# Zeros written by VectorE for the idle products, six early scores in a group, and products in the first four places of the first round

## The chip, the cores and the metric

The kernel runs on one core of one Trainium2 chip. Its time is the device time of one execution in microseconds. Engines are named as in the profile: PE is TensorE (PEld its weight loads), DVE is VectorE, ACT is ScalarE, POOL is GpSimd, SP is SyncE, which issues the loads and stores.

## The reference

A layer norm, then full attention over 32 heads of width 16 and a bilinear gated network on the same normalised rows; their product is added to the input. S = 2048 tokens, D = 512, F = 1792, all in float32.

```
xn = layernorm(x)
q, k, v = split(xn @ wqkv)                  # 32 heads of 16
p = softmax(q k^T / 4);  s = (p v) @ wo
g = silu(((xn @ w_gate) * (xn @ w_up)) @ w_down)
out = x + s * g
```

## The kernel before

Products are split: each float32 operand is cut into a high and a low part, and three products (high-high, high-low, low-high) are summed, so a 128x512 tile with a depth of 512 takes twelve matmuls. The kernel has three stages.

**Start and early stage** (`early`, line 707 on). Four tiles of x are loaded and normalised, transposed on TensorE (`ln_turn`, L246), and K, Q and V are projected from them (`full`, L267). To have something on TensorE while the first tiles are being normalised there are *idle products*, `warm` (L730): matmuls of the identity with a tile of zeros named `acc`, four ahead of the first transposes and three between the first and the second transposes. A float32 matmul shows as two in the trace, hence eight and six. The identity and the zeros are written by POOL, the zeros last of its set-up.

The 252 projection products of the early stage run as one stream, numbered by `n`. At some values of `n` other work is put in: statistics, normalisations, transposes of the remaining x tiles, and, by the table `EARLY`, *early scores* (`score`, L610 and L612). A score is a matmul of a 48-row piece of Q with K into one bank of PSUM; two scores that follow each other lie in the lower and the upper half of the array. VectorE then takes the maximum of each row of the bank (`TENSOR_REDUCE mx<-s`). Scores of a query block must all be done before its exponentials; 64 of them make a block, after which `maxima` reduces them once more (L616 to L621) and stores them. In all 86 scores (`LEAD`) run in the early stage, so that the scores stay 86 ahead of the exponentials from there on. The banks of this stage are four for scores (tag `s`), two for transposes and idle products (`x`), two for projections (`f`).

**Main part.** It is a chain of *places* (`position`). In a place stand one product for an exponential (`expo`, t, L632; ScalarE takes the exponential, L634) and one score (L610). After eight places or so, as the loop at the end of `body` decides, follows a *block* of weighted values (`block`, pv, L645). Between the places the *filler* puts other products (the rest of the projections, the gated network), as pairs of half-array matmuls (`pair`, L286 and L290). `spread(n)` shares the products of a round out to n gaps, `part` issues one gap's share. In the main part three banks (`s`) hold scores, three (`st`) hold t and pv, two (`misc`) the filler's sums.

The first round differs: four places stand ahead of the loop, without filler; the loop's first turn adds eight more, with the filler's share in six gaps. Then comes the first block.

**End** (`ending`): the output projection, the gate, the sum and the stores.

What sets the order: TensorE, ScalarE, VectorE and GpSimd execute in the order in which the program is written (a manual schedule), with waits only on data and on banks. SP issues all transfers from one queue, in program order.

Of the kernel before, what the change touches and what calls it, by code (L numbers as in the profile page):

```python
# [11 lines left out]
F32 = mybir.dt.float32  # L12
# [7 lines left out]
P = 128  # L20
# [11 lines left out]
LEAD = 86  # L32
CYCLES = 240
AHEAD = range(1, 5)
# [2 lines left out]
EBUFS = 11  # L37
HBUFS = 2
QBUFS = 2
EARLY = [66, 75, 84, 93] + [104 + 37 * n // 4 for n in range(17)]  # L40
EARLY_BUFS = {"s": 4, "x": 2, "f": 2}
BUFS = {"st": 3, "s": 3, "misc": 2}
LOWER, UPPER = slice(0, 64), slice(64, P)
# [5 lines left out]
def body(ctx, tc, x, wqkv, wo, wg, wu, wd, out):  # L49
    nc = tc.nc  # L50
    x = x.rearrange("b s d -> (b s) d")
# [19 lines left out]
    pool, sync = Tied(nc.gpsimd), Tied(nc.sync)  # L71

    def dma(dst, src):
        sync.dma_start(dst, src)
# [5 lines left out]
    keep = ctx.enter_context(tc.tile_pool(name="keep", bufs=1))  # L80
# [6 lines left out]
    OD = [dram.tile([H, 32, 512], F32, name=f"OD{c}") for c in range(NC)]  # L87
    YD = [dram.tile([P, 4, D], F32, name=f"YD{c}") for c in range(NC)]

    ident = keep.tile([P, P], F32, name="ident")  # L90
    make_identity(nc, ident)
    ks = [keep.tile([P, 2, S], F32R, name="ks0")]
# [9 lines left out]
    def ones_columns(tts):  # L102
        pool.memset(V[:, tts, DH:H * VW:VW], 1.0)
        pool.memset(V[:, tts, H * VW:], 1.0)

    ones_columns(slice(0, 8))
    idle = keep.tile([P, 512], F32, name="acc", bufs=2)
    pool.memset(idle, 0.0)

    fst = {}  # L110

# [5 lines left out]
    def psum(tag, name):  # L117
        ps, bufs = fst["ps"]
        return ps.tile([P, 512], F32, tag=tag, name=name, bufs=bufs[tag])
# [28 lines left out]
    def etile():  # L148
        return ep.tile([P, 512], F32, name="e", bufs=EBUFS)
# [15 lines left out]
    def wtile(name):  # L165
        return keep.tile([P, ND, P], F32 if name[-1] == "r" else F32R, name=name, bufs=1 if name[-1] == "r" else 2)
# [23 lines left out]
    def load_x(tt):  # L190
        dma(tokens(tt), x[tt * P:(tt + 1) * P])
# [406 lines left out]
            for pr in range(2):  # L598
                dma(k[b:b + 2, pr].bitcast(F32), ones)

    def score(n, other):

        i, r = divmod(n, 4 * NT)
        r, j = divmod(r, 4)
        j ^= other
        kc, t = divmod(r, 4)
        b, pr = 64 * (j % 2), j // 2
        k = ks[(i // NC) % 2]
        o = psum("s", f"s{i}_{r}_{j}")
        nc.tensor.matmul(o, QS[i][b:b + KB, pr, t * P:(t + 1) * P],  # L610
                         k[b:b + KB, pr, kc * 512:(kc + 1) * 512], start=True, stop=True)
        nc.vector.tensor_reduce(MX[i][:, j, t, kc:kc + 1], o, axis=AX.X, op=OP.max)  # L612
# [94 lines left out]
    def early():  # L707

        nc.scalar.activation(look, eps[0:1], AF.Sqrt)
        for tt in range(4):  # L710
            load_x(tt)
        wraw = []
        for which in (1, 0):
            wraw.append(wtile(f"w{which}r"))
            dma(wraw[-1], wqkv[:, which * D:which * D + P].rearrange("(d p) f -> p d f", p=P))
        norm["raws"] = raws = [etile() if d < 3 else part_tile() for d in range(ND)]
        for d in range(ND):
            dma(raws[d], wqkv[d * P:(d + 1) * P, 2 * D:])
        for tt in range(4, NT):
            load_x(tt)  # L720

        def ahead(m):
            fst["qk", m] = qk_weights(m, 1), qk_weights(m, 0)

        def exp_table(_):
            nc.scalar.activation(look, eps[0:1], AF.Exp)

        def warm(n):
            for _ in range(n):
                nc.tensor.matmul(psum("x", "warm"), ident, idle, start=True, stop=True)  # L730

        warm(4)
        first = (0, 1), (2, 3)
        for tts in first:
            ln_open(tts)
        ln_stats(0)
        ln_stats(1)
        ln_root(first[0])
        ln_scale(first[0])
        ln_apply(0)  # L740
        ln_apply(1)
        ln_stats(2)
        ln_stats(3)
        ln_turn(0)
        ln_turn(1)
        warm(3)
        ln_root(first[1])
        ln_scale(first[1])
        ln_apply(2)
        last = ln_apply(3)  # L750
        ln_low(0)
        ln_low(1)
        ln_turn(3)
        ln_turn(2)
        ln_low(3)
        ln_low(2)
        wk, wq = [split_raw(f"w{which}", raw, last) for which, raw in zip((1, 0), wraw)]
        wv = [[etile().bitcast(F32R) for _ in range(ND)] for _ in range(2)]
        for d in range(ND):
            nc.scalar.activation(wv[0][d], raws[d], AF.Copy)  # L760
            pool.tensor_tensor(wv[1][d], raws[d], wv[0][d], op=OP.subtract)

        def k(c):
            yield from qk_proj(wk, 0, 1, c, "f")
            load_k(0, [c])

        def q(c):
            yield from qk_proj(wq, 0, 0, c, "f" if c else "x")
            load_q(c)

        def v(*tts):
            for tt in tts:
                yield from v_proj(wv, tt, "f")

        at = {n: [] for n in range(253)}
        for c, stats, apply, turns in ((1, (0, 2, 4, 6), (26, 26, 26, 26), (38, 42, 46, 50)),
                                       (2, (16, 20, 26, 27), (60, 60, 62, 62), (70, 74, 79, 83)),
                                       (3, (30, 34, 36, 38), (73, 73, 85, 85), (100, 106, 112, 118))):
            for t in range(4):
                for n, fn in ((stats[t], ln_stats), (apply[t], ln_apply), (turns[t], ln_turn)):  # L780
                    at[n].append((fn, 4 * c + t))
        for tts, n, root, scale in ((tuple(range(4, 8)), 0, 13, 25), (tuple(range(8, NT)), 16, 52, 53)):
            at[n].insert(0, (ln_open, tts))
            at[root].append((ln_root, tts))
            at[scale].insert(0, (ln_scale, tts))
        at[190].append((ones_rows, ks[0]))
        at[150].append((exp_table, None))
        at[205].append((ahead, 1))
        at[130] += [(ones_columns, slice(8, NT)), (other_keys, None)]
        fst["v"] = v_proj(wv, NT - 1, "st")  # L790
        gens = [k(0), q(0), v(0, 1, 2), k(1), q(1), v(3), k(2), v(4, 5), k(3), v(*range(6, NT - 1))]
        scored = 0
        stream = (n for g in gens for n in g)
        for n in range(253):
            for fn, arg in at[n]:
                fn(arg)
            if n in EARLY:
                for _ in range(4 if n != EARLY[-1] else LEAD - scored):
                    score(scored, 0)
                    scored += 1  # L800
                if scored == 64:
                    maxima(0)
            next(stream, None)
        assert scored == LEAD
        return wq
# [132 lines left out]
    TOTAL = NU * NT * 4  # L938

    with tc.manual_schedule(engines=ORDERED):  # L940
        with banks_of(EARLY_BUFS):
            fil = Filler(filler(early()), spread)
        ctx.enter_context(banks_of(BUFS))
        run(fst["v"])
        q = 0
        while q < 4:
            position(q)
            q += 1
        for b in range(NU * NT // 2):
            if fil.done:  # L950
                parts = iter([3, 2, 3, 2, 2, 2, 1, 2])
                fil = Filler(ending(), lambda n: next(parts))
            work = fil.begin()
            if b >= NU * NT // 2 - 2:
                last = TOTAL - 4 * (NU * NT // 2 - 1 - b)
            else:
                fits = min(9, max(7, int(2.6 + 0.62 * work))) if q + LEAD < TOTAL and work else 8
                need = 8 * (b + 1)
                last = min(max(q + fits, need + AHEAD[0]), need + AHEAD[-1], TOTAL - 4)
            count = last - q  # L960
            fil.spread(max(2, count - 2))
            for k in range(count):
                if k == count - 1:
                    run_all(gates)
                position(q)
                q += 1
                if 0 < k < count - 1 or count < 3:
                    fil.part()
            if b < NU * NT // 2 - 1:
                values([ready.pop(2 * b), ready.pop(2 * b + 1)])  # L970
        run_all(before_values)
        run_all(gates)
        while heads:
            step_small(heads)
        block([ready.pop(NU * NT - 2), ready.pop(NU * NT - 1)])
        run_all(behind_values)
        flush()
        while fil.left or not fil.done:
            now[0] += 1
            prepare()  # L980
            if not fil.left:
                fil.fetch()
            for _ in range(fil.left):
                next(fil.gen)
            fil.left = 0
            fil.fetch()
            flush()
# [17 lines left out]
```

## Time and profile before

| | us |
|---|---|
| median of three runs | 1714.24 (1713.63 to 1714.4) |
| the profiled execution, whole | 1715.28 |
| its span | 1713.4 |
| first idle product | 2.70 |
| first transposes on TensorE | 9.05 |
| first early scores | 31.80 |
| first place of the main part | 102.50 |
| first block of weighted values | 109.65 |

The times in the trace count from the start of the span. A row of the timeline reads: start, length (both in us), engine, line and operation, written tile and read tiles, shape, count, and in brackets how long the engine had been idle before it and what it waited for. Consecutive instructions of one kind are merged into one row with their count. The length of a matmul in the trace is longer than the distance to the next one, since matmuls overlap; so the pace of TensorE is read from the distances between starts.

### The profile page before, as it was taken

How to read it: one execution, taken by the hardware profiler on the slowest of the kernel's cores; microseconds unless marked ns; L12 is line 12 of the kernel's file. 1: busy time of each engine (PE TensorE's matmuls, PEld its weight loads, DVE VectorE, ACT ScalarE, POOL GpSimd, SP SyncE). 2: the span in 40 equal slices, each digit the busy share in tenths (PEclk: the TensorE clock that was granted, in tenths of full speed). 3: DMA queues.
4: the chain of work that ended last, by engine and by line, in shares of the span. 5: the costliest groups of instructions: out<-in, count | busy, mean ns of one | idle time of the engine just before them, and what ended most of it. 6: DMA issues, size and time to landing. Idle time of an engine off the chain costs nothing. (4 is left out here: it accounts for less than half of the span.)

```text
span 1713.4 us, 35012 instructions
## 1 busy us (share of the span) xinstructions
PE 1701.9 (99%) x13574; PEld 1043.7 (61%) x13574; DVE 1430.9 (84%) x2478; ACT 1309.0 (76%) x2568; POOL 884.9 (52%) x890
## 2 busy tenths in 40 slices
PE   8999999999999999999999999999999999999998
PEld 5666656666666666666656665666666566666655
DVE  6788888888888888888888888888888888888933
ACT  6357777777877778788777887877778787777774
POOL 5314444763653647446354572663637546446672
PEclk9999999999999999999999999999999999999999
DMA  6316633620241222412115220330225112011352
GB/s 209 108 40 193 248 126 117 153 72 13 71 91 36 82 72 67 96 41 61 36 49 136 65 72 24 87 76 27 60 84 122 54 36 73 27 54 47 123 178 78
DMA packets 117378, 145.79 MB, mean 85 GB/s; under 512 B 12636, under 2 KB 74332, under 8 KB 114524
## 3 DMA queue, kind: packets, MB, share of 16 engines
q1 hardware_dynamic: 117212, 143.55, 29.0%
q8 instruction: 107, 1.75, 0.4%
q14 instruction: 59, 0.48, 0.1%
HBM read 95.94 MB, written 47.45 MB: 84 GB/s over the span
## 5 line engine op out<-in xcount | busy, mean ns | idle before, releaser
L612 DVE TENSOR_REDUCE mx<-s 128x1 f32<-128x512 f32 x2048 | 1256.1, 683 | 212.4 <-PE s L610 178.1
L634 ACT ACTIVATE e<-t 128x512 f32<-128x512 f32 x2048 | 1101.3, 601 | 97.8 <-PE pv L645 46.6
L632 PE MATMUL t<-qs,ks 50*128 50x512 f32 x2048 | 782.3, 408 | 0.1
L610 PE MATMUL s<-ks,qs 48*128 48x512 f32 x2048 | 768.1, 409 | 0.6 <-DVE mx L612 0.5
L63 POOL TENSOR_TENSOR acc<-acc,part 128x512 f32<-128x512 f32 x214 | 276.1, 1290 | 588.8 <-ACT part L656 588.4
L632 PEld LDWEIGHTS t<-qs,ks 50*128 50x128 f32 x2048 | 359.2, 185 | 270.7 <-issue 110.2
L645 PE MATMUL pv<-e,V 128*32 128x512 f32 x4096 | 492.5, 598 | 0.0
L610 PEld LDWEIGHTS s<-ks,qs 48*128 48x128 f32 x2048 | 350.8, 185 | 28.2 <-issue 5.6
L656 ACT ACTIVATE part<-pv 128x512 f32<-128x512 f32 x214 | 128.1, 599 | 205.1 <-PE pv L645 205.1
L645 PEld LDWEIGHTS pv<-e,V 128*32 128x32 f32 x4096 | 107.0, 109 | 242.3 <-issue 216.9
L290 PE MATMUL g<-fh,w1h 64*128 64x512 f32 x224 | 90.5, 404 | 0.0
L286 PE MATMUL u<-fh,w0h 64*128 64x512 f32 x224 | 90.5, 404 | 0.0
L290 PE MATMUL y<-dh,hh 64*128 64x512 f32 x224 | 89.5, 400 | 0.0
L286 PE MATMUL y<-dh,hh 64*128 64x512 f32 x224 | 88.9, 397 | 0.0
L290 PE MATMUL u<-fh,w0l 64*128 64x512 f32 x224 | 88.2, 394 | 0.0
L290 PE MATMUL g<-fl,w1h 64*128 64x512 f32 x224 | 88.1, 393 | 0.0
L286 PE MATMUL u<-fh,w0l 64*128 64x512 f32 x224 | 88.0, 393 | 0.0
L290 PE MATMUL g<-fh,w1l 64*128 64x512 f32 x224 | 88.0, 393 | 0.0
L286 PE MATMUL g<-fl,w1h 64*128 64x512 f32 x224 | 88.0, 393 | 0.0
L286 PE MATMUL g<-fh,w1h 64*128 64x512 f32 x224 | 87.9, 392 | 0.0
L290 PE MATMUL u<-fl,w0h 64*128 64x512 f32 x224 | 87.8, 392 | 0.0
L286 PE MATMUL g<-fh,w1l 64*128 64x512 f32 x224 | 87.8, 392 | 0.0
(262 smaller groups left out, 2982.7 us busy)
## 6 DMA issues: line engine op xcount, KB each, us to landing
w1r<-in_wg_dram SPq DMA_DIRECT2D x56, 256.0 KB
w0r<-in_wu_dram SPq DMA_DIRECT2D x56, 256.0 KB
wdr<-in_wd_dram SPq DMA_DIRECT2D x56, 256.0 KB
qs<-QD SPq DMA_DIRECT2D x64, 192.0 KB
ks<-KD SPq DMA_DIRECT2D x12, 768.0 KB
KD<-hl SPq DMA_DIRECT2D x16, 512.0 KB
QD<-hl SPq DMA_DIRECT2D x16, 512.0 KB
OD<-acc SPq DMA_DIRECT2D x31, 256.0 KB
```

The source lines that it names most:

```text
L63: got = getattr(self.engine, name)(*args, **kw)
L286: nc.tensor.matmul(outs[k], l[LOWER], r[LOWER], start=k == 0 and n == 0, stop=(stop or k == 0) and n == len(low) - 1, skip_group_check=k == 1)
L290: nc.tensor.matmul(outs[1 - k], l[UPPER], r[UPPER], start=k == 0 and m == 0, stop=(stop or k == 0) and m == len(high) - 1, skip_group_chec ...
L610: nc.tensor.matmul(o, QS[i][b:b + KB, pr, t * P:(t + 1) * P], k[b:b + KB, pr, kc * 512:(kc + 1) * 512], start=True, stop=True)
L612: nc.vector.tensor_reduce(MX[i][:, j, t, kc:kc + 1], o, axis=AX.X, op=OP.max)
L632: nc.tensor.matmul(o, k[b:b + KR, pr, kt * P:(kt + 1) * P], QS[i][b:b + KR, pr], start=True, stop=True)
L634: nc.scalar.activation(e, o, AF.Exp, scale=DH ** -0.5)
L645: nc.tensor.matmul(o[32 * j:32 * j + 32], V[:, kt, h0:h0 + 32], es[j], start=n == 0, stop=n == len(todo) - 1)
L656: nc.scalar.activation(part, o, AF.Copy)
```

## The change

Three edits.

1. The tile of zeros is written by VectorE as the first thing in the program, no longer by POOL, and the idle products use it for both operands, where the identity was one of them.
2. The table of early scores: up to product 113 it stays as it was; then six scores at 124, at 142 and at every 13th product after that up to 233, and four each at 246 and 251, where there were four at about every ninth product and six at 252. The first two scores of a group of six use the banks tagged `x`. The call of `maxima` goes into the loop over a group, so that it comes directly behind score 64 also where that lies inside a group.
3. The four places without filler ahead of the main loop are gone. The loop's first turn has all twelve places, and spreads the filler's products over ten gaps.

```
-EARLY = [66, 75, 84, 93] + [104 + 37 * n // 4 for n in range(17)]
+EARLY = {66: 4, 75: 4, 84: 4, 93: 4, 104: 4, 113: 4, 124: 6, **{142 + 13 * n: 6 for n in range(8)}, 246: 4, 251: 4}
...
+    idle = keep.tile([P, 512], F32, name="acc", bufs=2)
+    nc.vector.memset(idle, 0.0)
     ident = keep.tile([P, P], F32, name="ident")
...
-    idle = keep.tile([P, 512], F32, name="acc", bufs=2)
-    pool.memset(idle, 0.0)
...
-    def score(n, other):
+    def score(n, other, tag="s"):
...
-        o = psum("s", f"s{i}_{r}_{j}")
+        o = psum(tag, f"s{i}_{r}_{j}")
...
-                nc.tensor.matmul(psum("x", "warm"), ident, idle, start=True, stop=True)
+                nc.tensor.matmul(psum("x", "warm"), idle[:, 0:P], idle, start=True, stop=True)
...
             if n in EARLY:
-                for _ in range(4 if n != EARLY[-1] else LEAD - scored):
-                    score(scored, 0)
+                for m in range(EARLY[n]):
+                    score(scored, 0, "x" if m < EARLY[n] - 4 else "s")
                     scored += 1
-                if scored == 64:
-                    maxima(0)
+                    if scored == 64:
+                        maxima(0)
...
         q = 0
-        while q < 4:
-            position(q)
-            q += 1
         for b in range(NU * NT // 2):
...
-                last = min(max(q + fits, need + AHEAD[0]), need + AHEAD[-1], TOTAL - 4)
+                last = min(max(q + fits, need + AHEAD[0]), need + AHEAD[-1], TOTAL - 4) if b else need + AHEAD[-1]
```

How the order on TensorE changes is seen best at three places. In the names, s is a bank of scores (query block, tile and head follow in its name), v and p are projections, t is the product for an exponential. First, the middle of the early stage, before:

```order
L610 MATMUL s_10_0_824<-ks_132,qs 128x512
L610 MATMUL s_10_1_827<-ks_132,qs 128x512
L610 MATMUL s_10_2_830<-ks_132,qs 128x512
L610 MATMUL s_10_3_833<-ks_132,qs 128x512
L267 MATMUL v_820<-e,xh_152 128x512 x5
L267 MATMUL v_820<-e,xl_156 128x512 x4
L610 MATMUL s_11_0_845<-ks_132,qs 128x512
L610 MATMUL s_11_1_848<-ks_132,qs 128x512
L610 MATMUL s_11_2_851<-ks_132,qs 128x512
L610 MATMUL s_11_3_854<-ks_132,qs 128x512
```

and of the change:

```order
L610 MATMUL s_9_0_806<-ks_134,qs 128x512
L610 MATMUL s_9_1_809<-ks_134,qs 128x512
L610 MATMUL s_9_2_812<-ks_134,qs 128x512
L610 MATMUL s_9_3_815<-ks_134,qs 128x512
L610 MATMUL s_10_0_818<-ks_134,qs 128x512
L610 MATMUL s_10_1_821<-ks_134,qs 128x512
L267 MATMUL v_793<-e,xl_156 128x512
L267 MATMUL v_826<-e,xh_152 128x512 x8
L267 MATMUL v_826<-e,xl_156 128x512 x4
L610 MATMUL s_10_2_839<-ks_134,qs 128x512
L610 MATMUL s_10_3_842<-ks_134,qs 128x512
```

Where four scores stood between nine products, six stand between thirteen. Second, the end of the early stage on TensorE, before:

```order
L267 MATMUL v_1047<-e,xh_154 128x512 x6
L267 MATMUL v_1047<-e,xl_158 128x512 x4
L610 MATMUL s_4_0_1072<-ks_132,qs 128x512
L610 MATMUL s_4_1_1075<-ks_132,qs 128x512
L610 MATMUL s_4_2_1078<-ks_132,qs 128x512
L610 MATMUL s_4_3_1081<-ks_132,qs 128x512
L610 MATMUL s_5_0_1084<-ks_132,qs 128x512
L610 MATMUL s_5_1_1087<-ks_132,qs 128x512
L267 MATMUL v_1095<-e,xh_154 128x512 x8
L267 MATMUL v_1095<-e,xl_158 128x512 x4
```

and of the change:

```order
L610 MATMUL s_4_0_1066<-ks_134,qs 128x512
L610 MATMUL s_4_1_1069<-ks_134,qs 128x512
L267 MATMUL v_1053<-e,xh_154 128x512 x2
L267 MATMUL v_1053<-e,xl_158 128x512 x3
L610 MATMUL s_4_2_1077<-ks_134,qs 128x512
L610 MATMUL s_4_3_1080<-ks_134,qs 128x512
L610 MATMUL s_5_0_1083<-ks_134,qs 128x512
L610 MATMUL s_5_1_1086<-ks_134,qs 128x512
L267 MATMUL v_1053<-e,xl_158 128x512
L267 MATMUL v_1095<-e,xh_154 128x512 x8
L267 MATMUL v_1095<-e,xl_158 128x512 x4
```

The stage ended with six scores and twelve products; it now ends with two groups of four (the last two scores of the first are shown), five products apart, and thirteen products. Third, the first places of the main part on TensorE, before:

```order
L632 MATMUL t_0_0_1109<-qs,ks_132 128x512
L610 MATMUL s_5_3_1113<-ks_132,qs 128x512
L632 MATMUL t_0_1_1116<-qs,ks_132 128x512
L610 MATMUL s_5_2_1120<-ks_132,qs 128x512
L632 MATMUL t_0_2_1123<-qs,ks_132 128x512
L610 MATMUL s_6_1_1127<-ks_132,qs 128x512
L632 MATMUL t_0_3_1130<-qs,ks_132 128x512
L610 MATMUL s_6_0_1134<-ks_132,qs 128x512
L632 MATMUL t_1_0_1137<-qs,ks_132 128x512
L610 MATMUL s_6_3_1141<-ks_132,qs 128x512
```

and of the change:

```order
L632 MATMUL t_0_0_1109<-qs,ks_134 128x512
L610 MATMUL s_5_3_1113<-ks_134,qs 128x512
L632 MATMUL t_0_1_1116<-qs,ks_134 128x512
L610 MATMUL s_5_2_1120<-ks_134,qs 128x512
L286 MATMUL p_0_2_1123<-xh_153,w0h 128x512
L290 MATMUL p_0_3_1124<-xh_154,w0h 128x512
L286 MATMUL p_0_2_1123<-xl_157,w0h 128x512
L290 MATMUL p_0_3_1124<-xl_158,w0h 128x512
L632 MATMUL t_0_2_1129<-qs,ks_134 128x512
L610 MATMUL s_6_1_1133<-ks_134,qs 128x512
```

The filler's pairs (L286, L290) now begin behind the second place instead of the sixth. From the first block of weighted values on, and on ScalarE and SP throughout, the order is the same as before; on VectorE and POOL only the memset has changed sides.

## The prediction

> **What bounds the kernel now.** I read the page's table of engines first, then the busy time by stretches.
>
> ```profile
> span 1713.4 us, 35012 instructions
> PE 1701.9 (99%) x13574; PEld 1043.7 (61%) x13574; DVE 1430.9 (84%) x2478; ACT 1309.0 (76%) x2568; POOL 884.9 (52%) x890
> 0.00:10.00 10.00, 7.30 (x17) 3.61 (x18) 4.54 (x14) 2.90 (x5) 2.00 (x12) 1.00 0.86 275
> 140.00:1600.00 1460.00, 1460.00 (x12022) 891.21 (x12020) 1271.23 (x2182) 1160.05 (x2285) 779.39 (x775) 1.00 0.28 79
> ```
>
> In the rows by stretch the columns are length, then busy time and instructions of PE, PEld, DVE, ACT and POOL, the granted clock, the DMA share and GB/s. TensorE is busy for all of the 1460 us of the main part. Every row there starts relative to what ran before, and from the first weighted-values block on the order of the changed kernel is that of the old one on every engine. So what is won or lost before that block (about 110 us) should arrive at the end one to one. Busy does not mean fast, though: the three edits work on places where TensorE's matmuls stand farther apart than they have to. I go through these in order of time, on the timeline.
>
> **The start.** The idle products wait for zeros that POOL writes last of its set-up.
>
> ```profile
> 0.73 1.28 ACT L709 ACT_TABLE_LOAD   x1 [0.73 <-PEq L992]
> 2.11 0.53 POOL L63 MEMSET acc<- 128x512 f32 x1
> 2.70 6.52 PE L730 MATMUL warm<-acc,ident 128*128 128x512 f32 x8 [2.70 <-POOL acc L63]
> 3.45 0.70 DVE L204 BATCH_NORM_STATS2 st<-ks 128x6 f32<-128x512 f32 x1 [3.45 <-DMA ks<-in_x_dram]
> 6.51 0.81 ACT L235 ACTIVATE ks<-ks,mr,e 128x512 f32<-128x512 f32 x1 [1.02 <-DVE mr L220]
> 6.51 0.55 DVE L234 TENSOR_SCALAR ks<-ks,e,mr 128x512 f32<-128x512 f32 x1
> 7.12 0.34 PEld L730 LDWEIGHTS warm<-acc,ident 128*128 128x128 f32 x1 [0.52 <-issue]
> 7.98 0.34 PEld L730 LDWEIGHTS warm<-acc,ident 128*128 128x128 f32 x1 [0.52 <-issue]
> 8.62 0.14 PEld L246 LDWEIGHTS xT<-ident,ks 128*128 128x128 f32 x1 [0.31 <-issue]
> 9.05 1.04 PE L246 MATMUL xT<-ident,ks 128*128 128x128 f32 x8
> 9.93 2.74 PE L730 MATMUL warm<-acc,ident 128*128 128x512 f32 x6
> 12.57 1.09 PE L246 MATMUL xT<-ident,ks 128*128 128x128 f32 x8
> 12.58 0.61 POOL L63 CAST w1h<-w1r 128x512 fp32r<-128x512 f32 x1 [9.94 <-DVE ks L234]
> ```
>
> The normalised rows are ready at 6.51 + 0.81 = 7.32, but the transposes start at 9.05: TensorE is still in its first four idle products (eight matmuls). Their pitch is 7.98 - 7.12 = 0.86 us; the last step is 8.62 - 7.98 = 0.64, and from 9.93 on six take (12.57 - 9.93) / 6 = 0.44 at most. So TensorE runs at half speed until about 8.41 (0.43 us slow and 0.21 fast make that 0.64), 5.71 us after its first product.
>
> *Edit 1*, zeros from VectorE. VectorE has nothing to do before 3.45 and is released with the others at about 0.73. Its memset is not in the trace. Nearest rows: POOL's own, 0.53, and VectorE's 128x512 pass, 0.55; the bound below is 0.22 (VectorE's pass over 64 columns, quoted further down), the one above 0.70 (the statistics row). I take 0.55, so zeros at 1.28 and products from 1.33 with the same 0.05 us hand-over: 1.37 earlier. If the half speed lasts the same 5.71 us from the first product, everything on TensorE moves by 1.37, and the transposes start at 7.68, still behind the 7.32 of the data. Weights of zeros instead of the identity cost nothing by themselves: the loads have the same shape. POOL loses 0.53 us that nobody waits for (its next work is released at 12.58).
>
> After that the chain is transposes, ScalarE's copies, the second half of the normalisation, transposes at 12.57, first real products; each waits for the one before, so all of it moves. Of the rows above only the statistics at 3.45 wait for a load, and they stay where they are. Whether a later load, now wanted earlier, is late, no row of before can show: with the DMA engines 86% busy in the first ten us it is possible, and it is the bound at 0. Term 1: **-1.37**, between 0 and -1.68 (transposes right at the data, 7.37).
>
> [...]
>
> **The stage of products and early scores** (31 to 102.5 us). A group of four scores between products:
>
> ```profile
> 85.39 0.73 PE L610 MATMUL s<-ks,qs 48*128 48x512 f32 x4
> 86.05 0.50 PE L267 MATMUL v<-e,xl 128*128 128x512 f32 x1
> 86.39 1.99 PE L267 MATMUL v<-e,xh 128*128 128x512 f32 x8
> 87.99 0.39 PE L267 MATMUL v<-e,xh 128*128 128x512 f32 x1
> 88.30 0.73 PE L610 MATMUL s<-ks,qs 48*128 48x512 f32 x4
> 118.24 0.49 PE L632 MATMUL t<-qs,ks 50*128 50x512 f32 x1
> 118.58 0.40 PE L632 MATMUL t<-qs,ks 50*128 50x512 f32 x1
> 118.81 0.39 PE L286 MATMUL p<-fh,w1h 64*128 64x512 f32 x1
> ```
>
> Products inside a run are (87.99 - 86.39) / 7 = 0.23 us apart. The last before a group takes 88.30 - 87.99 = 0.31, the first behind it 0.34, and the group's two pairs (two scores side by side) 0.66 instead of 0.46. Each change between whole-array products and half-array scores thus costs some 0.08 + 0.11 + 0.20 = 0.39 us a group, whatever the group's length, provided an inner pair takes 0.23. The rows at 118 say so: behind the change the first pair takes 0.34, the next 0.23.
>
> *Edit 2*. From product 122 on there were 14 groups of four and one of six; now there are nine of six and two of four, 62 scores both ways. Four groups fewer: 4 x 0.39 = -1.56. If the inner pair took 0.34 instead, the nine groups of six would give back 9 x 0.11 = 0.99. The two extra scores use banks that the transposes have left by then.
>
> The price to watch is VectorE, which empties each bank.
>
> ```profile
> 85.30 0.22 DVE L616 TENSOR_REDUCE mm<-mx 128x16 fp32r<-128x64 f32 x1
> 86.03 2.44 DVE L612 TENSOR_REDUCE mx<-s 128x1 f32<-128x512 f32 x4
> 94.68 2.48 DVE L612 TENSOR_REDUCE mx<-s 128x1 f32<-128x512 f32 x4 [0.42 <-PE s L610]
> 97.82 3.68 DVE L612 TENSOR_REDUCE mx<-s 128x1 f32<-128x512 f32 x6 [0.66 <-PE s L610]
> 97.29 0.73 PE L610 MATMUL s<-ks,qs 48*128 48x512 f32 x4
> 98.57 1.09 PE L610 MATMUL s<-ks,qs 48*128 48x512 f32 x2 [0.54 <-DVE mx L612]
> 99.59 2.08 PE L267 MATMUL v<-e,xh 128*128 128x512 f32 x8
> 103.08 7.38 DVE L612 TENSOR_REDUCE mx<-s 128x1 f32<-128x512 f32 x12 [1.57 <-PE t L632]
> ```
>
> Maxima follow each other every (3.68 - 2.48) / 2 = 0.60 us. A new period is thirteen products and six scores: 13 x 0.23 + 3 x 0.23 + 0.39 = 4.07 us, against 6 x 0.60 = 3.60 on VectorE; it keeps up. The row of small maxima (85.30 to 86.03, 0.73) now falls inside a group of six, so that VectorE is 4.33 in that one period, and the next group's late scores wait about 0.3. At the end, groups 246 and 251 have only five products between them: 0.66 + 0.34 + 3 x 0.23 + 0.31 = 2.0 us for four maxima of 2.4. The first group's fourth maximum ends 0.53 + 0.68 + 3 x 0.60 = 3.01 after that group's start (0.53 being 97.82 - 97.29); the second group's last score, whose turn is at 2.0 + 0.34, waits some 0.7. The old end waited too: its group of six lasted 99.59 - 97.29 = 2.30 instead of 0.34 + 0.23 + 0.32 = 0.89, a loss of 1.41. So waits go from 1.4 to about 1.1 to 1.2. Term 2: -1.56 - 0.25, **-1.8**, between -0.5 (inner pairs dear, no wait saved) and -2.5.
>
> **The first round.** Twelve places (an exponential's product t and a score s) stood before the first weighted-values block, the first four without products, the rest with all twelve pairs.
>
> ```profile
> 102.50 0.50 PE L632 MATMUL t<-qs,ks 50*128 50x512 f32 x1
> 104.30 0.49 PE L632 MATMUL t<-qs,ks 50*128 50x512 f32 x1
> 105.02 0.49 PE L610 MATMUL s<-ks,qs 48*128 48x512 f32 x1
> 105.62 0.50 PE L610 MATMUL s<-ks,qs 48*128 48x512 f32 x1
> 109.33 0.40 PE L610 MATMUL s<-ks,qs 48*128 48x512 f32 x1
> 109.65 1.92 PE L645 MATMUL pv<-e,V 128*32 128x512 f32 x16
> 112.08 5.15 DVE L612 TENSOR_REDUCE mx<-s 128x1 f32<-128x512 f32 x8 [1.62 <-PE s L610]
> ```
>
> The first places go at VectorE's pace (105.62 - 105.02 = 0.60), with TensorE half empty; then products crowd the rest, 109.33 - 105.62 = 3.71 for five places. *Edit 3* gives places 1 to 10 their share. TensorE's work is then about 12 x 0.23 + 12 x 0.23 = 5.5 us, and VectorE's pace decides: the first maximum starts 0.58 after the round and a score follows the maximum three before it, so the last score stands at 0.58 + 0.68 + 0.07 + 8 x 0.60 = 6.13 us, the block at 6.13 + 0.32 = 6.45. It stood at 109.65 - 102.50 = 7.15. Term 3: **-0.70**, between 0 and -1.0. The idle 1.62 us on VectorE behind the block shrinks; it is nobody's wait.
>
> **Sum.** -1.37 - 1.8 - 0.70 = -3.9 us. The profiled execution spans 1713.4 and took 1715.28 in all; the median of the other runs is 1714.24, with three runs 0.8 us apart. The span would become 1709.5, the median 1714.24 - 3.9 = **1710.4**.
>
> **Rivals.**
> - [...] Chance 0.20. [...]
> - *The clock opens at 8.41 whenever the products start.* Eight slow matmuls take 9.05 - 2.70 + 0.64 = 6.99 (the last 0.64 ran at double speed), so from 1.33 they end at 8.32 and term 1 is -0.73. For: one opening cannot tell a fixed moment from a fixed delay. Sum -3.2, 1711.0. Chance 0.16.
> - *The groups of six save little*: inner pairs at 0.34, or VectorE behind. Against: the rows at 118 and the 3.60 of 4.07. Sum -2.9, 1711.3. Chance 0.17.
> - *Slower*: with zeros on both sides the idle products no longer count as work, and the clock stays at half until real products have run 5.71 us. The first eight then end at 8.32, eight transposes take 1.76 instead of 9.93 - 9.05 = 0.88, six idle products 6 x 0.86 = 5.2, and the second transposes end near 17.0 instead of 13.45 (+3.5); at half speed for 5.71 us more another 2.85 are lost. +6.4 against -2.5 from terms 2 and 3: 1718.1. Against: the streamed operand was zero before, so every product was zero already, and the clock came. It decides if the transposes start after about 12. Chance 0.05.
>
> The forecast has 0.42. What a measurement here can tell from no change is about 0.2%, 3.4 us, so the bar for faster is 1710.8: forecast and first rival are beyond it (0.62), the next two lie within (0.33), the last is slower (0.05). The range takes in both middle rivals and half the bounds of the terms: 1709.0 to 1712.6.
>
> **What would show it.** Right: first idle product near 1.33, transposes before 7.7, groups of six taking about 0.89 from first score to next product, TensorE waiting for VectorE only near the end of the stage, and the first weighted-values block some 3.9 us earlier than 109.65, the distance then kept to the end. Wrong: an idle-product pitch of 0.86 beyond 8.4 us, waits for maxima in every group of six, or a distance at 110 us that the main part loses again.

## The result and the profile after

| | before | after |
|---|---|---|
| median of 21 runs each, us | 1714.01 | 1712.22 |
| lowest and highest | 1713.2 to 1714.97 | 1710.68 to 1714.51 |
| ratio, 95% interval | | 0.9988, [0.9983, 0.9994] |
| the profiled execution, whole | 1715.28 | 1711.65 |
| its span | 1713.4 | 1709.9 |

The change is faster by 1.8 us, a little under half of the 3.9 that the prediction had, and so within the 0.2% that stood for no change. The two lines of the table do not tell the same thing, though: in the profiled executions the span fell by 3.5 us. The runs of after say why a median and a profile can differ here; sorted, in us:

```
1710.68 .71 .74 .77 .79 .80 .81 .87 | 1711.65 | 1712.21 .22 .22 .33 .50 .64 .68 .70 | 1713.11 1713.79 1714.31 1714.51
```

Eight runs lie near 1710.8 (the forecast was 1710.4), eight near 1712.4, four higher. The 21 runs of before are one heap, 1.8 us wide. So the first question is not why the change gave too little, but what about half of its executions lose.

First the execution that was profiled, part by part. The timeline of its start:

```profile
0.91 0.48 DVE L91 MEMSET acc<- 128x512 f32 x1 [0.91 <-PEq L989]
1.45 6.78 PE L730 MATMUL warm<-acc 128*128 128x512 f32 x8 [1.45 <-DVE acc L91]
6.56 0.81 ACT L235 ACTIVATE ks<-ks,mr,e 128x512 f32<-128x512 f32 x1 [1.02 <-DVE mr L220]
6.74 0.34 PEld L730 LDWEIGHTS warm<-acc 128*128 128x128 f32 x1 [0.52 <-issue]
7.59 0.19 PEld L246 LDWEIGHTS xT<-ident,ks 128*128 128x128 f32 x1 [0.52 <-issue]
8.06 1.04 PE L246 MATMUL xT<-ident,ks 128*128 128x128 f32 x8
```

The idle products start at 1.45 (2.70 before), but the transposes only 0.99 earlier, at 8.06 (9.05): the pitch of the idle products is still 7.59 - 6.74 = 0.85 at the end, so nearly all eight ran at half speed (0.43 is the pitch at full speed, 6.23 - 5.80 in the weight loads of the change's repeat below). The granted clock reads 1.00 over the first ten us, before and after, so it does not show the half speed; the pitch of the products and of their weight loads does. The data would have been there at 6.56 + 0.81 = 7.37.

The timeline of the early stage, on TensorE:

```profile
60.12 0.96 PE L610 MATMUL s<-ks,qs 48*128 48x512 f32 x6
61.01 0.73 PE L267 MATMUL p<-xl,w1h 128*128 128x512 f32 x2
84.40 1.55 PE L610 MATMUL s<-ks,qs 48*128 48x512 f32 x6
85.88 1.19 PE L267 MATMUL v<-e,xh 128*128 128x512 f32 x4
95.11 1.55 PE L610 MATMUL s<-ks,qs 48*128 48x512 f32 x4
96.59 0.50 PE L267 MATMUL v<-e,xl 128*128 128x512 f32 x1
99.77 0.50 PE L632 MATMUL t<-qs,ks 50*128 50x512 f32 x1
106.31 1.92 PE L645 MATMUL pv<-e,V 128*32 128x512 f32 x16
```

A group of six takes 61.01 - 60.12 = 0.89, as predicted. Two groups wait for VectorE: the one behind the small maxima (85.88 - 84.40 = 1.48 instead of 0.89) and the last (96.59 - 95.11 = 1.48 instead of 0.66). The first place stands at 99.77, 2.73 earlier than before; the first block at 106.31, 3.34 earlier; the span ends 3.5 earlier. So this execution won 0.99 at the start, 1.74 in the early stage and 0.61 in the first round, and kept it to the end.

### The profile page after: what moved, and what is told of

Its sections match the earlier page's. It is cut to its first block, busy times and chain, and to the rows that moved or that the text cites. A ratio compares the mean times of both kernels' runs of the same rounds, so it can differ in the third digit from the quotient of the medians.

```text
span 1709.9 us, 35015 instructions
## 1 busy us (share of the span) xinstructions
PE 1700.0 (99%) x13574; PEld 1043.2 (61%) x13574; DVE 1430.8 (84%) x2479; ACT 1308.5 (77%) x2568; POOL 888.2 (52%) x889
## 3 DMA queue, kind: packets, MB, share of 16 engines
q8 instruction: 107, 1.75, 0.4%
## 5 line engine op out<-in xcount | busy, mean ns | idle before, releaser
L63 POOL TENSOR_TENSOR acc<-acc,part 128x512 f32<-128x512 f32 x214 | 279.8, 1308 | 582.5 <-ACT part L656 582.0
L290 PE MATMUL g<-fh,w1h 64*128 64x512 f32 x224 | 90.5, 404 | 0.0
L286 PE MATMUL u<-fh,w0h 64*128 64x512 f32 x224 | 90.4, 404 | 0.0
L290 PE MATMUL y<-dh,hh 64*128 64x512 f32 x224 | 89.6, 400 | 0.0
L286 PE MATMUL y<-dh,hh 64*128 64x512 f32 x224 | 88.8, 397 | 0.0
L290 PE MATMUL u<-fh,w0l 64*128 64x512 f32 x224 | 88.2, 394 | 0.0
L290 PE MATMUL g<-fl,w1h 64*128 64x512 f32 x224 | 88.0, 393 | 0.0
L286 PE MATMUL g<-fl,w1h 64*128 64x512 f32 x224 | 88.0, 393 | 0.0
L286 PE MATMUL u<-fh,w0l 64*128 64x512 f32 x224 | 88.0, 393 | 0.0
L290 PE MATMUL g<-fh,w1l 64*128 64x512 f32 x224 | 88.0, 393 | 0.0
L286 PE MATMUL g<-fh,w1h 64*128 64x512 f32 x224 | 87.9, 392 | 0.0
L290 PE MATMUL u<-fl,w0h 64*128 64x512 f32 x224 | 87.8, 392 | 0.0
L286 PE MATMUL y<-dl,hh 64*128 64x512 f32 x224 | 87.8, 392 | 0.0
```

Of the source, the lines that this page charges most:

```text
L63: got = getattr(self.engine, name)(*args, **kw)
L286: nc.tensor.matmul(outs[k], l[LOWER], r[LOWER], start=k == 0 and n == 0, stop=(stop or k == 0) and n == len(low) - 1, skip_group_check=k == 1)
L290: nc.tensor.matmul(outs[1 - k], l[UPPER], r[UPPER], start=k == 0 and m == 0, stop=(stop or k == 0) and m == len(high) - 1, skip_group_chec ...
```

## The experiments

All were timed in five rounds (11 runs), beside the kernel before on the same chip, on three chips in all. The theories go by a letter in the expectations. **G**: the moment in the first ten us at which TensorE's products go from half to full pace (from 0.86 to 0.43 us apart; in the prediction and the expectations, the moment at which its clock opens) differs between executions, and that alone makes the heaps. **S**: the scatter comes with the groups of six, VectorE and the banks. **Z**: zeros as weights change something (the pace, the loads). **F** came later, from the profiles of the first four runs: a fetch of instructions delays a store of K, and a score in the group at product 142 waits for it; **F1** is F with the addition that the order up to product 131 decides where the fetch comes.

### Edit 1 alone

```
+    idle = keep.tile([P, 512], F32, name="acc", bufs=2)
+    nc.vector.memset(idle, 0.0)
     ident = keep.tile([P, P], F32, name="ident")
...
-                nc.tensor.matmul(psum("x", "warm"), ident, idle, start=True, stop=True)
+                nc.tensor.matmul(psum("x", "warm"), idle[:, 0:P], idle, start=True, stop=True)
```

> The kernel before with edit 1 alone (zeros by VectorE, zeros as both operands, everything else as it was). Theory G (the clock of TensorE: idle products that begin at 1.45 let the full clock come at very different moments from run to run, and in some runs take it away again ahead of the real products): the runs scatter over some 3 to 4 us, as those of the changed kernel do, the fastest about 1.3 us below the kernel before (near 1712.5), the slowest above all of it (1716 or more), the median between -0.5 and +1 us of the kernel before. Theory S (the scatter belongs to the groups of six, VectorE and the banks): the scatter is that of the kernel before, under 2 us, and the median 1.0 to 1.3 us lower.

Measured: 1713.66 (1713.0 to 1714.1) against 1714.44, ratio 0.9995 [0.9986, 1.0004]. One heap, 1.1 us wide: the start alone does not make the two heaps, so G falls as their cause. The median gain is 0.8, not 1.37, and the interval takes in no gain at all. In the profile, idle products start at 1.45 as in after, but the transposes wait for ScalarE's row until 7.97, since a load of x came late:

```profile
4.75 0.69 DVE L204 BATCH_NORM_STATS2 st<-ks 128x6 f32<-128x512 f32 x1 [0.42 <-DMA ks<-in_x_dram]
7.97 1.07 PE L246 MATMUL xT<-ident,ks 128*128 128x128 f32 x8 [0.83 <-ACT ks L235]
```

### Edits 2 and 3, without edit 1

```
-    idle = keep.tile([P, 512], F32, name="acc", bufs=2)
-    nc.vector.memset(idle, 0.0)
...
     ones_columns(slice(0, 8))
+    idle = keep.tile([P, 512], F32, name="acc", bufs=2)
+    pool.memset(idle, 0.0)
...
-                nc.tensor.matmul(psum("x", "warm"), idle[:, 0:P], idle, start=True, stop=True)
+                nc.tensor.matmul(psum("x", "warm"), ident, idle, start=True, stop=True)
```

> The changed kernel with edit 1 undone (zeros by POOL, identity as weights), so edits 2 and 3 alone. The profile of the changed kernel shows 1.7 us won in the early stage and 0.6 in the first round. Theory G: a median 2.3 us below the kernel before (near 1711.7), scatter under 2 us as that of the kernel before, so faster than the changed kernel's 1712.2. Theory S: the scatter stays at 3 to 4 us and the median is 1.0 to 1.3 us above the changed kernel's.

Measured: 1713.58 (1711.71 to 1714.27), ratio 0.9992 [0.9983, 1.0001]. The spread is back, 2.6 us: it comes with edits 2 and 3, and the median lies near what S expected, 1.4 above the changed kernel's (on another chip). And the profiled execution (1714.27) shows a wait that neither before nor after has. TensorE's timeline at product 142:

```profile
61.31 0.49 PE L610 MATMUL s<-ks,qs 48*128 48x512 f32 x2
62.52 0.46 PE L610 MATMUL s<-ks,qs 48*128 48x512 f32 x1 [0.71 <-DMA ks<-KD]
63.25 0.70 PE L610 MATMUL s<-ks,qs 48*128 48x512 f32 x3 [0.27 <-DVE mx L612]
```

The third score of the group, the first that needs the third quarter of K, starts 1.21 behind the first pair and the fourth another 0.73 later; in after all six scores are over in 0.89. So it is a load that a score waits for here, and not only VectorE and the banks as S has it.

### After, with the zeros again by POOL

Only the memset goes back to POOL's place in the program; both operands stay zeros.

> The changed kernel with the zeros written by POOL again, at the old time (2.64), but still zeros as both operands. Theory G: it is the early start that counts, so as the run with edit 1 undone: near 1711.7, scatter under 2 us. Theory Z (products of zeros with zeros count less as work than those with the identity): scatter of 3 to 4 us and a median of 1712.5 or more.

Measured: 1713.01 (1711.3 to 1713.6), ratio 0.9988 [0.9979, 0.9997], three runs near 1711.4, one at 1712.25, seven from 1712.87 up. Beside the run with the identity as weights (0.9992) no difference can be told: Z has nothing for it. (At half pace a load of weights takes 0.34 us with the identity, at 7.12 in before, and 0.34 with zeros, at 6.74 in after.) G's 1711.7 is missed as well. The profile has the wait at the third score too.

### After, with six idle products ahead

```
-        warm(4)
+        warm(6)
```

> The changed kernel with six idle products instead of four ahead of the first transposes, so that TensorE has no gap between them and the transposes even where the full clock comes early. Theory G with the gap as its cause: transposes between 8.4 and 10.1 us, that is 0.5 us later than in the kernel before; median near 1712.2, scatter under 2 us, no run above 1713.5. If the gap is not the cause, runs above 1713.5 stay, and the median rises by about 1 us to 1713.2.

Measured: 1712.33 (1711.83 to 1713.16), ratio 0.9988 [0.9979, 0.9997]. One heap, 1.3 us wide, higher than after's low heap; the transposes stand at 8.10, earlier than expected but 0.70 later than in the repeat of the change below (7.40). It looked like support for G, but the profile shows another thing: the fetch of instructions that is the subject of the next run lies between 48.6 and 51.6 us here, ahead of the store at 52.91. So this run does not tell G from F.

### The change once more

No edit: a second set of executions, with a profile of its own.

> The changed kernel unchanged, for its scatter and a second profile. [...] Theory G (clock): the times spread evenly over 4 us and the profile of a slow one shows a late or a second opening of the clock.

Measured: 1712.16 (1711.38 to 1714.86), ratio 0.9987 [0.9979, 0.9996]; six runs up to 1712.16, five from 1712.91 up. The two groups are less clearly apart than in the first set. The profiled one took 1712.91 and has the wait. The timeline of this execution: SP's queue (its store of the K quarter, then the load of it), then TensorE at product 142:

```profile
52.27 0.81 SPq L63 DMA_DIRECT2D KD<-hl  x2
57.64 0.79 SPq L63 DMA_DIRECT2D ks<-KD  x2
59.55 0.49 PE L610 MATMUL s<-ks,qs 48*128 48x512 f32 x2
60.64 0.46 PE L610 MATMUL s<-ks,qs 48*128 48x512 f32 x1 [0.59 <-DMA ks<-KD]
61.53 0.70 PE L610 MATMUL s<-ks,qs 48*128 48x512 f32 x3 [0.43 <-DMA ks<-KD]
62.16 0.73 PE L267 MATMUL p<-xl,w1h 128*128 128x512 f32 x2
```

The same two rows of SP's queue in after's profiled execution:

```profile
52.85 0.81 SPq L63 DMA_DIRECT2D KD<-hl  x2
56.16 0.79 SPq L63 DMA_DIRECT2D ks<-KD  x2
```

From the store to the load it is 57.64 - 52.27 = 5.37 us here and 56.16 - 52.85 = 3.31 there (before: 3.30). TensorE's six scores last 62.16 - 59.55 = 2.61 instead of 0.89: 1.72 us lost. The two scores that wait start 3.00 and 3.89 us behind the load's issue. In after the third score stood at about 60.12 + 0.34 = 60.46, 4.30 behind the issue: the two halves of the load had 1.3 and some 0.4 us to spare, and 2.06 us more on the store uses that up.

What goes with the late store is in the view of the DMA engines. First after, 51 to 57 us, in 40 slices of 0.15 us (busy share in tenths, GB/s), then the queue of instruction fetches (packets, MB, share):

```profile
DMA  0004000000000000009999999989997000000000
GB/s 0 0 0 109 0 0 0 0 0 0 0 0 0 0 0 0 0 27 410 410 437 437 437 437 410 437 301 410 382 410 287 14 0 0 0 0 0 0 0 0
q8 instruction: 1, 0.02, 1.1%
```

and the repeat of it, 52 to 58 us:

```profile
DMA  0000000799999998999920040000000000000000
GB/s 0 0 0 0 0 0 0 328 437 410 410 437 382 437 437 314 369 396 396 355 82 14 14 123 0 0 0 0 0 14 0 0 0 0 0 0 0 0 0 0
q8 instruction: 1, 0.02, 1.0%
```

Each window holds one fetch of 16 KB (0.15 us at 109 GB/s are 16 KB). In after it lies at 51.45, ahead of the store's packets, which then run through. In the repeat it lies at 55.45 in the store's tail: the store thins out to 14 GB/s, the fetch comes, and a lone last packet of the store follows 0.9 us behind it. SP issues the load only when the store is complete; its waits in that stretch (51 to 60 us; total, times, longest), first here, then in after:

```profile
SPq L63 <- DMA KD<-hl: 4.5, 1, 4.5
SPq L63 <- DMA KD<-hl: 2.4, 1, 2.4
```

Over all eleven profiles it goes together without exception: where the fetch falls into that tail (the runs without edit 1, with POOL's zeros, this one, and the next) the store-to-load distance is 5.35 to 5.37 us; in the other seven, where it comes ahead of the store, 3.30 or 3.31. In those four the fetch lies 3.1 to 3.3 us behind the store's issue; in the seven it lies ahead of it, by 1.3 to 1.9 us in six and by 1.3 to 4.3 in the one with six idle products ahead, and in none in between. That is hardly chance: a fetch that was itself held back by the store's packets would look the same, and which delays which is not shown.

### The quarter wanted later

Only the first two of the six scores at product 142 stay there. The third, the first to need the late load, moves ten products on, to 152: from 59.60 + 0.34 = 59.94 to 62.52 in the profile below. The groups behind it move too, and one group of six ends the stage instead of two of four.

```
-EARLY = {66: 4, 75: 4, 84: 4, 93: 4, 104: 4, 113: 4, 124: 6, **{142 + 13 * n: 6 for n in range(8)}, 246: 4, 251: 4}
+EARLY = {66: 4, 75: 4, 84: 4, 93: 4, 104: 4, 113: 4, 124: 6, 142: 2, **{n: 6 for n in (152, 165, 178, 190, 202, 214, 226, 238, 249)}}
```

> The changed kernel with another table from product 142 on: two scores at 142, six each at 152, 165, 178, 190, 202, 214, 226, 238 and 249, so that the first score on K's third quarter comes at product 152 instead of 142 (2.8 us later), and the stage ends with six scores over six banks instead of twice four. Theory F: one heap, no run more than 1.5 us above the fastest, median near 1710.4 (lower heap of the changed kernel, less about 0.5 us of waiting at the end), so some 1.5 us below the changed kernel's median. Theory G: the scatter of 3 to 4 us stays, median about 0.5 us below the changed kernel's.

Measured: 1711.08 (1710.75 to 1711.28), ratio 0.9978 [0.9969, 0.9987]. One heap, 0.5 us wide; all its eleven runs lie below all eleven of the unchanged kernel on that chip. The timeline of its profiled execution (SP's queue, TensorE):

```profile
52.33 0.81 SPq L63 DMA_DIRECT2D KD<-hl  x2
57.69 0.79 SPq L63 DMA_DIRECT2D ks<-KD  x2
59.60 0.49 PE L610 MATMUL s<-ks,qs 48*128 48x512 f32 x2
60.02 0.74 PE L267 MATMUL p<-xl,w1h 128*128 128x512 f32 x2
62.52 0.96 PE L610 MATMUL s<-ks,qs 48*128 48x512 f32 x6
63.41 1.18 PE L267 MATMUL v<-e,xl 128*128 128x512 f32 x4
85.94 1.75 PE L610 MATMUL s<-ks,qs 48*128 48x512 f32 x6
87.61 0.73 PE L267 MATMUL v<-e,xl 128*128 128x512 f32 x2
94.14 1.17 PE L610 MATMUL s<-ks,qs 48*128 48x512 f32 x6
95.25 0.95 PE L267 MATMUL v<-e,xl 128*128 128x512 f32 x3
```

The load is as late as in the repeat (5.36 behind the store), and nobody waits: the six scores at 62.52 take 0.89. An execution with the late load, and it was the fastest of the eleven. So a late load costs nothing where no score wants it early, and the second heap goes with that wait: the upper heap was the wait for K's third quarter. Not all of the gain is this, though. The last four rows show that the waits for maxima are 1.67 - 0.89 = 0.78 and 1.11 - 0.89 = 0.22, 1.00 in all, where after has 1.41 (see term 2 below): some 0.4 us come from the new end of the stage. This version gains 3.75 us at the median, less than the 1710.4 that was expected of it, by another sum than the forecast's for the change, and its median lies below those of both kernels on that chip.

### Edit 3 alone

```
         q = 0
-        while q < 4:
-            position(q)
-            q += 1
...
-                last = min(max(q + fits, need + AHEAD[0]), need + AHEAD[-1], TOTAL - 4)
+                last = min(max(q + fits, need + AHEAD[0]), need + AHEAD[-1], TOTAL - 4) if b else need + AHEAD[-1]
```

> The kernel before with edit 3 alone (products in the first four places). By the prediction's third term 0.70 us faster, by the profile of the changed kernel 0.62, with the kernel before's scatter; the profile shows the first weighted-values block 6.5 us after the first place instead of 7.15. If VectorE's pace had already bound all twelve places, no difference.

Measured: 1713.58 (1713.12 to 1714.71) against 1714.83, ratio 0.9994 [0.9985, 1.0004]; no second heap. The median gain, 1.25, is twice what was expected, and the interval takes in both that and nothing. The profile sizes it better than eleven runs do; TensorE's timeline, first place and first block:

```profile
101.19 0.50 PE L632 MATMUL t<-qs,ks 50*128 50x512 f32 x1
107.72 1.92 PE L645 MATMUL pv<-e,V 128*32 128x512 f32 x16
```

107.72 - 101.19 = 6.53, against 7.15 before: -0.62.

### Old order up to product 131

Groups of four up to 131 as before, then nine of six from 142 on, so that the score in question is the first at 142.

```
+EARLY = {**{n: 4 for n in (66, 75, 84, 93, 104, 113, 122, 131)}, **{n: 6 for n in (142, 160, 178, 190, 202, 214, 226, 238, 249)}}
```

> The changed kernel with the old groups of four up to product 131 (so four at 122 and at 131 instead of six at 124), then six each at 142, 160, 178, 190, 202, 214, 226, 238 and 249. As many groups as the run with the later quarter, but the first score on K's third quarter stands at 142 again, now as the first of its group. Theory F1 (the group of six at 124 draws TensorE's instruction fetch into the store; with groups at 113 and 122 it comes ahead of the store): one heap, median near 1711.1, scatter under 1 us, and the fetch in the profile 3 us or more ahead of the store's end. Theory F2 (the fetch falls into the store in some executions whatever the table): two heaps again, 1711.0 and 1.5 us or more above, median 1712 or more.

Measured: 1711.67 (1711.35 to 1712.36), ratio 0.9983 [0.9974, 0.9992]. One heap, 1.0 us wide, 0.6 above the median that F1 expected, and the profile has the fetch at 50.6, ahead of the store; the load follows the store by 3.31. Its single heap is what F1 says: with the old order up to there the fetch keeps out of the way (in the four profiles of such kernels), with six scores at 124 it does in three of seven. It is a count, not a mechanism: what moves the fetch was not found.

### The later quarter, without edit 1

The table of the run with the later quarter, with POOL's zeros and the identity, as in the second experiment.

> The run with the later quarter, but with the zeros from POOL at the old time and the identity as weights: what edit 1 is worth where no wait for K's third quarter hides it. [...] By the prediction's count from the first product: 1.37 us above it with the same scatter.

Measured: 1711.86 (1711.34 to 1712.66) against 1714.75, ratio 0.9983 [0.9974, 0.9992]. 2.9 us below its before, where the same with edit 1 is 3.75 below: edit 1 is worth some 0.9 at the median here, not the 1.37 of the prediction's count (two chips, and intervals wider than the difference), and the spread goes from 1.3 to 0.5 us with it.

## Why the prediction held where it did, and where it failed

**The number.** In the profiled execution the terms came out at -0.99, -1.74 and -0.61 where -1.37, -1.8 and -0.70 were forecast: the places and the kinds of gain were right. The median is another matter. It lies inside the range (1709.0 to 1712.6) but short of the 1710.8 that the forecast thought would more likely than not be passed (0.62), and what took the difference, the wait for a load in half of the executions and the scatter of the start, was in none of the sums. That it fell inside all the same is in part luck: the range had been opened for other rivals. Of the 0.62, 0.20 stood on full pace at an earlier, fixed moment; no run shows such a step, and what the runs show is full pace between 2.86 and 6.22 us behind the first product (term 1).

**Term 1, the start: right in kind, too large.** It gave -0.99 in after's profile instead of -1.37. The memset starts at 0.91, not 0.73, so products begin at 1.45 instead of 1.33. That is a tenth. The rest is the step "if the half speed lasts the same 5.71 us from the first product". It does not. The moment of full speed can be read from the loads of weights, which are 0.86 apart at half speed (7.98 - 7.12, before) and 0.43 at full (6.23 - 5.80, the change once more): the first step between two loads that is shorter than 0.86 contains it, at the step's start + 2 x step - 0.86. Loads on TensorE in the repeat of the change, in the run of edit 3 alone, and in the run with six idle products ahead, two to four rows each:

```profile
5.03 0.34 PEld L730 LDWEIGHTS warm<-acc 128*128 128x128 f32 x1 [0.52 <-issue]
5.80 0.19 PEld L730 LDWEIGHTS warm<-acc 128*128 128x128 f32 x1 [0.44 <-issue]
6.23 0.19 PEld L730 LDWEIGHTS warm<-acc 128*128 128x128 f32 x1 [0.24 <-issue]
7.40 1.06 PE L246 MATMUL xT<-ident,ks 128*128 128x128 f32 x8 [0.15 <-ACT ks L235]
```

```profile
5.43 0.32 PEld L730 LDWEIGHTS warm<-acc,ident 128*128 128x128 f32 x1 [0.52 <-issue]
5.99 0.19 PEld L730 LDWEIGHTS warm<-acc,ident 128*128 128x128 f32 x1 [0.24 <-issue]
7.70 1.04 PE L246 MATMUL xT<-ident,ks 128*128 128x128 f32 x8
```

```profile
4.17 0.26 PEld L730 LDWEIGHTS warm<-acc 128*128 128x128 f32 x1 [0.52 <-issue]
4.67 0.19 PEld L730 LDWEIGHTS warm<-acc 128*128 128x128 f32 x1 [0.24 <-issue]
```

| profile | first product | full speed at | later by |
|---|---|---|---|
| before | 2.70 | 7.98 + 2 x 0.64 - 0.86 = 8.40 | 5.70 |
| after | 1.45 | 7.59 + 2 x 0.47 - 0.86 = 7.67 | 6.22 |
| the change once more | 1.45 | 5.03 + 2 x 0.77 - 0.86 = 5.71 | 4.26 |
| edit 3 alone | 2.71 | 5.43 + 2 x 0.56 - 0.86 = 5.69 | 2.98 |
| six idle products ahead | 1.45 | 4.17 + 2 x 0.50 - 0.86 = 4.31 | 2.86 |

So the delay changes from execution to execution, by up to 6.22 - 2.86 = 3.36 us, for the same first product too (1.45: 2.86, 4.26, 6.22). The profiles of the later quarter (5.88 + 2 x 0.67 - 0.86 = 6.36, 4.91 behind 1.45) and of the same without edit 1 (7.14 + 2 x 0.62 - 0.86 = 7.52, 4.81 behind 2.71) lie between these ends. The forecast took one execution of before, an unlucky one, and after's own profile was unluckier still.

The transposes also have a floor: in the repeat they wait for ScalarE's row and start at 7.40, and a late load of x puts that floor at 7.97 in the run of edit 1 alone (the forecast had such a load as the bound at 0 of this term). After's profiled execution had its transposes at 8.06, 0.66 behind the repeat's; if the low heap starts as the repeat did, that is most of the 0.85 by which its 1711.65 stands above that heap. Edit 1 gains much where full pace comes late and little where it comes early (edit 3's run has the old products and transposes at 7.70); a median gain of 0.8 to 0.9 fits that, but is not pinned down by eleven runs. The rival of a fixed moment, 8.41, fell with the same table, where full pace comes at 4.31 to 8.40.

What sets the moment of full pace is not shown, and that the half speed is the clock's was the author's reading: the granted clock reads 1.00 over the first ten us, before and after.

**Term 2, the groups of six: the size was right, the waits were not.** Predicted -1.8, measured -1.74 where no load is late. Inside, two errors cancel: waits for maxima stayed at 0.59 + 0.82 = 1.41, as before, where 0.25 less was forecast (the two waits that the forecast names, 0.3 and 0.7, would even make 1.0, not its 1.1 to 1.2), and the four groups fewer gave 1.74 / 4 = 0.43 each instead of 0.39, if all that was won is theirs. The step of the forecast that left out what cost most is "The price to watch is VectorE, which empties each bank". It took banks and maxima for all that a score waits for. The group at 142 also reads a quarter of K that has just been through a store and a load, with some 0.4 us to spare for its second half. Before had the same little margin (61.53 - 57.19 = 4.34 us from the load's issue to its first use, the rows below), so the changed table did not spend it; but in all three profiles with before's table the fetch came early, and in four of the seven with six scores at 124 it fell on the store. That costs 1.7 us in about half of the executions (by the heaps), and takes the median from the low heap to the next.

```profile
53.89 0.81 SPq L63 DMA_DIRECT2D KD<-hl  x2
57.19 0.79 SPq L63 DMA_DIRECT2D ks<-KD  x2
61.53 0.73 PE L610 MATMUL s<-ks,qs 48*128 48x512 f32 x4
```

**Term 3, the first round: right.** Predicted -0.70, measured -0.62 alone and -0.61 in the change.

**That the distance is kept to the end: right.** 3.34 at the first block, 3.5 at the end of the span.

**The other rivals.** Groups of six that save little: no (-1.74). Slower, by zeros that do not count as work: no; with zeros on both sides full pace came at 7.67 in after, 5.71 in its repeat, 4.31 with six idle products ahead and 6.36 with the later quarter. None of the rivals named K's load or times in two heaps; the one load that the forecast thought of was at the start.

**What stays open.** What decides where the fetch of instructions comes, in an execution and in an order; whether the fetch holds up the store's last packet, or the store the fetch, or something else both (the fetch was moved with the order, never by itself); and after's four slowest runs, above 1713.1, of which no profile was taken.

## What to carry to other kernels

Before an instruction that reads loaded data is moved, or the order ahead of it changed, write down when its load was issued, when it lands, and the margin; engines and buffers are only half of what it waits for, and here a store and load through memory wanted some 2 us to spare (2.06 was the delay). Look at the list of times, not at the median alone: here two heaps were an event that some executions have (a wait of 1.72 us in the one profiled), and a profile shows one of them; take a second profile from the other heap. A price that hangs on the moment of full pace, read from one execution, was one draw out of a range of 3.36 us here (2.86 to 6.22 behind the first product).

## What the hardware showed that was not expected

Fetches of instructions go through the core's DMA engines, as the data do: the queue q8 moved 1.75 MB in 107 packets, 16 KB each, in before as in after. Their number keeps step with TensorE's matmuls, not with VectorE's instructions (before, 500 to 1000 us: 32 fetches, 4120 matmuls, 751 on VectorE; 1650 to 1713 us: 4, 440 and 36), so they are taken here to be TensorE's. Where one fell into the tail of a store, the load that waits for that store was issued 5.37 us behind it instead of 3.31. Its place differs between executions of one kernel (51.45, ahead of the store, and 55.45, inside it).

TensorE went from half to full pace 2.86 to 6.22 us behind the first product, in kernels whose first products were alike, while the granted clock read 1.00 over the first ten us (before and after). With the early first product and a load that is not waited for, the times of the whole kernel spread over 0.5 us (11 runs) where those of before spread over 1.6 on that chip (27 runs).
